# A list scheduler gets a model of two transfer queues and more slack behind transfers; the last stage's inputs lie on every second partition; the last rows are summed from PSUM

## The chip, the cores and the metric

One core of a Trainium2 chip runs the kernel. The metric is the device time of one execution in microseconds (us); the time before is the median of three runs.

## The reference

Input `x` is one sequence of 2048 rows with 512 channels. The result mixes two functions of it by a gate per row. `a` is a long convolution (an S4D state-space kernel of 128 complex states per channel, applied by a Fourier transform of twice the length), `b` is a bilinear feed-forward layer of inner width 1792 on a second input of the same shape.

```python
g = _sigmoid((x * gate_w).sum(-1, keepdims=True))
# a:
dt = jnp.exp(log_dt)
A = -jnp.exp(log_A_real) + 1j * A_imag
C = (C_real + 1j * C_imag) * dt[:, None]
P = jnp.exp((A * dt[:, None])[:, :, None] * pos[None, None, :])
K = 2.0 * jnp.einsum("dn,dnl->dl", C, P).real
y = irfft(rfft(u_t, 2 * L) * rfft(K, 2 * L), 2 * L)[:, :, :L]
a = y + u * D_skip
# b:
b = ((x_b @ w_gate) * (x_b @ w_up)) @ w_down
return g * a + (1 - g) * b
```

## The kernel before

**The feed-forward layer** is cut into 14 slices of 128 inner columns, in four groups (3, 3, 4 and 4 slices), and the rows into four chunks of 512. `hidden(f)` makes the two products `pg` and `pu` of a slice (12 TensorE matmuls each, since each operand is split into a high and a low part: `whi`, `wlo`, `xs`), copies `pg` to `h` (ScalarE), multiplies `h` by `pu` (VectorE, `h<-pu,h`), and splits the product into `hh` (ScalarE) and `hl` (VectorE). `down` adds the slices of a group up in a bank `y` of PSUM, one bank per 128 rows, two banks in all. `evacuate` scales `y` by 1 - g into `acc` (ScalarE) and adds it to the output in HBM (an accumulating transfer of the POOL queue). The weights of the next group come through two tiles `raw` (SP queue); ScalarE rounds each of them into `whi` or `dhi`, which frees the tile.

**The convolution** runs beside it on four quarters of the channels (`q`, 0 to 3), and its transform is a chain of small matmuls into banks `k`, with a trip through HBM between its steps because the data have to change partitions:

- `k_block(b)`, 16 blocks of 32 channels: VectorE builds two tables, `x` and `v`, by complex products (with squares `sq` from ScalarE); the last instruction of a block's tables is `v<-v,sq` of 32 by 8 elements per partition. Then the **kernel product** `k<-v,x` on TensorE makes the convolution kernel of these channels.
- `k_first(q)`: first step of the kernel's transform, matmuls `k<-kt,w1k_t`, stored to `sk_d`.
- `m_second`, four times per quarter: `m_load` fetches parts of `su_d` (the input's transform, made early on by `u_part` with matmuls `k<-in,w2s`) and of `sk_d` on the POOL queue; matmuls `k<-in,w2s`; ScalarE empties the banks into `ev`. `m_product` multiplies the two spectra on VectorE (`y<-ev`, `ev<-ev`, `y<-y,ev`). `m_inverse` takes two such products back (`k<-y,w3s`) and stores to `y_d` (SP queue).
- `m_last(q, gs)`: loads from `y_d` (`in<-y_d`, and `x<-y_d` in the last quarter), matmuls `k<-in,w_t` or `k<-x,w_t`, sums, the factor g, and an accumulating transfer into the output. The first four of the last chunk's row groups are kept apart: `ends()` reads their 4 x 128 output rows back into `sums` (`kt<-out`), adds the rest and stores them (`out<-kt`). These are the kernel's last instructions.

**The order of the work** is set by a list scheduler in the kernel's Python code. Every step is a task with an engine, a planned duration, inputs and outputs, a rank, for transfers a size, and for some an earliest time (`T_STEP` paces the slices). `Work.run` repeatedly takes the task that can start first by its plan, with ties by rank, and so writes out one fixed order per engine; on the chip each engine goes through its own list in that order and waits where an input is late. A transfer's end is planned in `run` by one `bus` for all transfers, which serves them one after the other at `DMA_RATE`; `ready` adds the lag between a task and its reader. `APART` keeps groups of small matmuls 6 us apart.

Every instruction is issued through one helper, so the profile gives all of them one line, L119; groups are told apart by the names of their tiles.

Of the kernel before, what the change touches and what calls it, by code (L numbers as in the profile page):

```python
# [18 lines left out]
P = 128  # L19
# [31 lines left out]
def fourier_matrices():  # L51

    k1, th = np.arange(64), 2 * np.pi / 4096

    def first(a, halves):
        re, im = np.cos(2 * np.pi * np.outer(a, k1) / 128), -np.sin(2 * np.pi * np.outer(a, k1) / 128)
        im[:, 0] = np.sin(np.pi * a)
        return np.concatenate([re, im, -re], axis=1)

    w1 = np.tile(first(np.arange(32) - 31.5, 2), (4, 1))  # L60
    rows = np.array(K_ROWS)
    w1k = np.tile(np.stack([first(2 * rows + b - 31.5, 1) for b in range(2)], 1), (4, 1, 1))
# [43 lines left out]
    w4 = w4.reshape(2, 2, 4, 2, 4, 32).transpose(0, 1, 3, 2, 4, 5)  # L106
    parts = (w1, w1k, w2.reshape(P, 32, 32), w3.reshape(P, 8, 2, 2, 64), w4.reshape(P, 32))
    return [np.ascontiguousarray(a, np.float32) for a in parts]

# [52 lines left out]
        self.deps, self.tiles, self.start, self.end, self.rows, self.many = set(), [], None, None, (), 0  # L162


class Work:


# [11 lines left out]


    APART, LESS = 6.0, 4.0
    DMA_RATE = 0.3

    def __init__(self):
        self.tags, self.tasks = {}, []
# [77 lines left out]
    def run(self):  # L263
# [4 lines left out]
        bus, order, known, rows, apart = 0.0, [], {}, {}, -9.0  # L268
# [51 lines left out]
def gated_mix_kernel(  # L320
# [260 lines left out]
    def evacuate(gi, ci, r, y):  # L581
        t = 4 * ci + r
        final = gi == len(GROUPS) - 1 and ci == LAST
        acc = new("glu", "raw", [P, D], bufs=2) if final and r == 3 else new("glu", "acc", [P, D], bufs=3)
        add(
            "act", 0.69, lambda: act.activation(acc.t, y.t, AF.Copy, scale=ngate[:, t : t + 1]),
            r=[y, (m_gate, ci)], w=[acc], rank=0,
        )
        if final:
            ending.append((r, acc))  # L590
        elif gi == 0:
            add("sp", 0.42, lambda: sp.dma_start(ov[:, t, :], acc.t), r=[acc], w=[(m_out, t)], dma=256)
        else:
            add(
                "pool", 0.95, lambda: pool_q.dma_start(ov[:, t, :], acc.t, accum_op=ALU.add),
                r=[acc, (m_out, t)], dma=640, rows=[t],
            )

    def ends():
# [2 lines left out]
        sums = new("tab", "kt", [P, 4, D])  # L602
        add(
            "sp", 0.42, lambda: sp.dma_start(sums.t, ov[:, t0 : t0 + 4, :]),
            r=[(m_y, (KT - 1, 0))], w=[sums, *((m_out, t0 + r) for r in range(4))], dma=1024, rows=range(t0, t0 + 4),
        )
        for r, acc in ending:
            t = t0 + r
            for q, (fin, parts) in late["fin"].items():
# [6 lines left out]
                    r=[*parts, (m_gate, LAST)], w=[(sums, (r, q))], rank=0,  # L616
                )
            add(
                "dve", 0.69,
                lambda r=r, acc=acc: dve.tensor_tensor(  # L620
                    out=sums.t[:, r], in0=acc.t, in1=sums.t[:, r], op=ALU.add
                ),
                r=[acc], w=[(sums, (r, q)) for q in range(KT - 2, KT)], rank=0,
            )
            add(
                "sp", 0.42, lambda r=r, t=t: sp.dma_start(ov[:, t, :], sums.t[:, r]), r=[(sums, (r, q)) for q in range(KT - 2, KT)], w=[(m_out, t)],
                dma=256, rank=-1,
            )
# [476 lines left out]
    def m_load(q, T):  # L1105
# [11 lines left out]
        for w, (src, m) in enumerate(((su_d, m_su), (sk_d, m_sk))):  # L1117
            for p in range(2):
# [6 lines left out]
                    r=[(m, (q, n0)) for n0 in range(0, 32, 8 if w else 4)], w=[(t, (T, w, p))], dma=256,  # L1125
                )
        return at, [(t, (T, w, p)) for w in range(2) for p in range(2)]

# [60 lines left out]
    def m_inverse(q, T0, ys, ws):  # L1189
# [27 lines left out]
            )  # L1217
        for h in range(2):
            st = sts[h]
            b0 = 32 * (T0 + h)  # L1220
            add(
                "sp", 0.42,
                lambda b0=b0, st=st: sp.dma_start(
                    y_d[q, b0 : b0 + 32].rearrange("(u a) n d -> (a n) u d", u=8),
                    st.t.rearrange("p t i j d -> p (t i j) d"),
                ),
                r=[st], w=[(m_y, (q, T0 + h))], dma=512,
            )


    def m_last(q, gs):

        banks, pieces, src = [[bank() for _ in range(2)] for _ in gs], [], []
        for g in gs:
            if q == KT - 1:
                t = late["y"][g]
            else:
                t = inp([P, 16, P])
                for p in range(2):
                    add(  # L1240
                        "sp", 0.42,
                        lambda t=t, g=g, p=p: sp.dma_start(
                            t.t[64 * p : 64 * p + 64],
                            y_d[q].rearrange("(k p) n d -> p k n d", p=2)[p, :, 16 * g : 16 * g + 16],
                        ),
                        r=[(m_y, (q, T)) for T in range(4)], w=[(t, p)], dma=512,
                    )
# [21 lines left out]
        for g, t, n0, n in pieces:  # L1269
# [30 lines left out]
            if n == 1 and n0 == LAST % 2:  # L1300
# [5 lines left out]
            add(  # L1306
                "pool", 0.95,
                lambda rs=rs, flat=flat: pool_q.dma_start(ov[:, rs[0] : rs[-1] + 1, cs], flat(), accum_op=ALU.add),
                r=[*parts, *((m_out, r) for r in rs)], dma=160 * len(rs), rows=rs,
            )  # L1310

    def transforms(q):
# [21 lines left out]
        if q == KT - 1:  # L1334
            late["y"] = [new("tab", "x", [P, 16, P], bufs=2) for _ in range(2)]
            for g in (1 - LAST // 2, LAST // 2):
                for half in range(2):
                    for p in range(2):
                        lanes = slice(64 * p + 32 * half, 64 * p + 32 * half + 32)
                        rows_y = y_d[q, 64 * half : 64 * half + 64].rearrange("(k p) n d -> p k (n d)", p=2)  # L1340
                        add(
                            "sp", 0.42,
                            lambda t=late["y"][g], lanes=lanes, rows_y=rows_y, p=p, g=g: sp.dma_start(
                                t.t[lanes], rows_y[p, :, 16 * P * g : 16 * P * g + 16 * P]
                            ),
                            r=[(m_y, (q, 2 * half + k)) for k in range(2)], w=[(late["y"][g], (half, p))], dma=256,
                        )
# [84 lines left out]
```

## Time and profile before

| | |
|---|---|
| median of 3 runs | 602.53 us (602.51 to 604.89) |
| the profiled execution, its own time | 601.78 us |
| its span | 600.0 us |
| mean granted TensorE clock | 0.994 |
| TensorE busy with matmuls | 585.8 us, 98% |
| VectorE, ScalarE busy | 512.3 us (85%), 401.0 us (67%) |
| moved by transfers | 137.33 MB, 229 GB/s on average |

The page gives busy time per engine, the share of busy time in 40 slices of the span, the transfers by queue, the chain of waits that ended last, and the costliest groups. A row of a group or of the timeline reads: engine, operation, output tile <- input tiles, shape, count, and in brackets how long the engine was idle before it and what released it. TensorE issues a 512-column matmul every 0.23 us, although each is listed with about 0.39 us, because they overlap.

### The profile page before, as it was taken

The page shows a single profiled execution, that of the slowest core. Times are in us where ns is not written, and L with a number is a line of the kernel's source. Part 1 is how long each engine was busy: PE and PEld are TensorE (multiplying, and loading weights), DVE is VectorE, ACT ScalarE, POOL GpSimd, SP SyncE. Part 2 cuts the span into 40 slices and gives each one's busy share as a digit, 9 for nine tenths or more (in the row PEclk, how much of TensorE's full clock was granted, in tenths as well). Part 3 has the DMA queues.
Part 4 walks back from the last instruction along what each step waited for, and adds up shares of the span by engine and source line. Part 5 has one row for each costly group of instructions (what it writes and reads, how often), then busy time and mean ns, then how long its engine had stood idle before and what let it go on. Part 6 is the DMA issues. An engine that isn't in the chain of part 4 may idle for free.

```text
span 600.0 us, 15878 instructions
## 1 busy us (share of the span) xinstructions
PE 585.8 (98%) x6500; PEld 443.4 (74%) x6500; DVE 512.3 (85%) x811; ACT 401.0 (67%) x893; POOL 128.9 (21%) x191
## 2 busy tenths in 40 slices
PE   8899999999999999999999999999999999999996
PEld 5657777777877787887777877866878777767674
DVE  6999999999998997999999999978999933486525
ACT  5279787999678479967959764979984423433522
POOL 0011212221204131310133301104353023201111
PEclk9989999999999999999999999999999999999998
DMA  8899979699869699996959945999999569959976
GB/s 276 314 357 340 336 281 338 187 207 253 232 175 227 166 241 248 195 229 163 302 135 266 215 129 171 226 250 239 182 203 260 95 159 355 244 153 264 279 141 122
DMA packets 71867, 137.33 MB, mean 229 GB/s; under 512 B 7156, under 2 KB 35828, under 8 KB 69364
## 3 DMA queue, kind: packets, MB, share of 16 engines
q1 hardware_dynamic: 47476, 88.21, 45.9%
q0 software_dynamic: 23904, 47.98, 40.4%
q8 instruction: 51, 0.84, 0.6%
q10 hardware_dynamic: 416, 0.13, 0.1%
q14 instruction: 20, 0.16, 0.1%
HBM read 81.25 MB, written 55.05 MB: 227 GB/s over the span
## 4 chain that ended last, share of the span: by engine, by line
PE 79%; DVE 8%; ACT 6%; DMA 5%; issue 1%; ACTq 0%; DVEq 0%
PE y L119 22%; PE pu L119 21%; PE pg L119 21%; PE k L119 15%; DMA raw<-in_wts 4%; DVE x L119 2%; DVE y L119 1%; DVE v L119 1%; ACT ts L119 1%; ACT whi L119 1%; DMA y<-in_xT 1%; ACT L119 1%; DVE h L119 1%; DVE t L119 1%; DVE xs L119 1%
## 5 line engine op out<-in xcount | busy, mean ns | idle before, releaser
L119 PE MATMUL pg<-xs,whi 128*128 128x512 f32 x448 | 139.2, 392 | 1.0 <-DVE xs L119 0.7
L119 PE MATMUL pu<-xs,whi 128*128 128x512 f32 x448 | 138.7, 391 | 0.0
L119 PEld LDWEIGHTS pg<-xs,whi 128*128 128x128 f32 x448 | 84.5, 189 | 20.0 <-ACT whi L119 2.0
L119 PEld LDWEIGHTS pu<-xs,whi 128*128 128x128 f32 x448 | 84.4, 188 | 17.1
L119 PE MATMUL y<-dhi,hl 128*128 128x512 f32 x224 | 90.5, 404 | 2.2 <-DVE x L119 1.1
L119 PE MATMUL pu<-xs,wlo 128*128 128x512 f32 x224 | 90.1, 402 | 0.9 <-issue 0.5
L119 PE MATMUL pg<-xs,wlo 128*128 128x512 f32 x224 | 90.1, 402 | 0.8 <-ACT whi L119 0.5
L119 PE MATMUL y<-dlo,hh 128*128 128x512 f32 x224 | 87.5, 391 | 1.3 <-DVE dlo L119 1.3
L119 PE MATMUL y<-dhi,hh 128*128 128x512 f32 x224 | 87.4, 390 | 0.0
L119 POOL DMA_DIRECT2D out<-acc x44 | 38.4, 954 | 184.8 <-ACT acc L119 173.8
L119 ACT COPY ev<-k 128x512 f32<-128x512 f32 x112 | 59.2, 595 | 15.7 <-PE k L119 15.6
L119 ACT CAST hh<-h 128x512 fp32r<-128x512 f32 x56 | 34.7, 620 | 43.3 <-DVE h L119 43.2
L119 ACT ACTIVATE acc<-y,ngate 128x512 f32<-128x512 f32 x63 | 42.8, 686 | 30.6 <-PE y L119 28.2
L119 DVE TENSOR_TENSOR h<-pu,h 128x512 f32<-128x512 f32 x56 | 38.6, 689 | 23.0 <-PE pu L119 22.2
L119 PEld LDWEIGHTS y<-dhi,hl 128*128 128x128 f32 x224 | 42.0, 188 | 21.7 <-issue 6.2
L119 PEld LDWEIGHTS pu<-xs,wlo 128*128 128x128 f32 x224 | 42.1, 188 | 19.2 <-issue 9.8
L119 PEld LDWEIGHTS pg<-xs,wlo 128*128 128x128 f32 x224 | 42.0, 188 | 19.1 <-issue 6.8
L119 ACT COPY h<-pg 128x512 f32<-128x512 f32 x56 | 33.1, 590 | 29.7 <-PE pg L119 27.8
L119 PEld LDWEIGHTS y<-dlo,hh 128*128 128x128 f32 x224 | 42.1, 188 | 9.5 <-DVE dlo L119 1.7
L119 PEld LDWEIGHTS y<-dhi,hh 128*128 128x128 f32 x224 | 42.1, 188 | 9.1
L119 DVE TENSOR_TENSOR hl<-h,hh 128x512 fp32r<-128x512 f32 x56 | 38.5, 687 | 8.4 <-ACT hh L119 8.4
L119 POOL DMA_DIRECT2D su_d<-ev x32 | 17.3, 549 | 90.2 <-ACT ev L119 90.2
(127 smaller groups left out, 1015.7 us busy)
## 6 DMA issues: line engine op xcount, KB each, us to landing
xs<-xs_d SPq DMA_DIRECT2D x36, 512.0 KB, 7.8
out<-acc POOLq DMA_DIRECT2D x44, 256.0 KB, 7.1
raw<-in_wts SPq DMA_DIRECT2D x36, 256.0 KB, 5.2
xs_d<-xs SPq DMA_DIRECT2D x16, 512.0 KB, 7.1
su_d<-ev POOLq DMA_DIRECT2D x32, 256.0 KB, 5.3
y_d<-ts SPq DMA_DIRECT2D x14, 512.0 KB, 6.5
in<-su_d POOLq DMA_DIRECT2D x24, 256.0 KB, 8.4
sk_d<-ev SPq DMA_DIRECT2D x6, 1024.0 KB, 6.2
```

The source lines that it names most:

```text
L119: got = getattr(self.engine, name)(*args, **kw)
```

## The change

Five things are edited.

1. The planner's transfers. `Bus` replaces the single `bus`: two queues, one for POOL and one for SP and ScalarE, each served in order, both at half the rate while both have work. `DMA_RATE` goes from 0.30 to 0.34, and times from issue to start (`SENT`) and from last byte to reader (`LANDED`) are given per queue. Sizes in the plan are set anew: 554 for 640 (`evacuate`), 476 for 256 (`m_load`), 203 for 160 per row group (`m_last`). None of these numbers is seen by the chip but through the order.
2. Slack: after 20 us of plan, a TensorE, ScalarE or VectorE task is planned no earlier than 1 us (`SURE`) after the transfer that it needs.
3. `y_d` rows lie on partitions another way: `w3` and `w4` are permuted on the host, `m_inverse` stores each staging tile by two transfers of 64 partitions (every second one), and the last stage's loads fill every second partition, with 64 each, where they filled 64 neighbouring ones (or 32 in the last quarter, which then has 4 loads of 512 KB for 8 of 256 KB). In quarters 0 to 2 a load now needs one half of the rows of `y_d`, stored by one `m_inverse` (`half`), where it needed all.
4. `ends()`: rows 2 and 3 of the last chunk are no longer copied to `acc` or `raw` by ScalarE; VectorE scales and adds them from PSUM in one instruction.
5. The very last row group is done in two halves of 256 columns, stored by SP and by the ScalarE queue.

```diff
+class Bus:
+    def __init__(self):
+        self.now, self.queues = 0.0, ([], [])
+
+    def serve(self, queues, now, until):
+        done = []
+        while now < until and any(queues):
+            share = sum(map(bool, queues))
+            step = min([q[0][1] * share for q in queues if q] + [until - now])
+            now += step
+            for q in queues:
+                if q:
+                    q[0][1] -= step / share
+                    if q[0][1] < 1e-6:
+                        done.append((q.pop(0)[0], now))
+        return done
...
-    DMA_RATE = 0.3
+    DMA_RATE = 0.34
+    SENT = {"sp": 0.9, "act": 0.9, "pool": 1.4}
+    LANDED = {"sp": 1.0, "act": 1.0, "pool": 1.3}
+    SURE = 1.0
...
         if d.engine == task.engine == "pe":
             return d.end
+        if d.dma and d.start > 20.0 and task.engine in ("pe", "act", "dve"):
+            return d.end + self.SURE
...
             if t.dma:
-                bus = max(bus, t.end + 1.3) + t.dma / self.DMA_RATE / 1000
-                t.end = bus + 0.5
+                for d, end in bus.add(t, t.end - 0.42 + self.SENT[t.engine], t.dma / self.DMA_RATE / 1000):
+                    d.end = end + self.LANDED[d.engine]
...
         final = gi == len(GROUPS) - 1 and ci == LAST
-        acc = new("glu", "raw", [P, D], bufs=2) if final and r == 3 else new("glu", "acc", [P, D], bufs=3)
+        if final and r > 1:
+            ending.append((r, y))
+            return
+        acc = new("glu", "acc", [P, D], bufs=3)
...
+            for n, cs in enumerate((slice(0, D // 2), slice(D // 2, D)) if r == 3 else (slice(0, D),)):
...
+                    scale = 1.0 if r < 2 else ngate[:, t : t + 1]
+                    dve.scalar_tensor_tensor(
+                        sums.t[:, r, cs], acc.t[:, cs], scale, sums.t[:, r, cs], op0=ALU.mult, op1=ALU.add
+                    )
+                e, q = ("act", act) if n else ("sp", sp)
...
-                    y_d[q, b0 : b0 + 32].rearrange("(u a) n d -> (a n) u d", u=8),
-                    st.t.rearrange("p t i j d -> p (t i j) d"),
+                        y_d[q, b0 : b0 + 16].rearrange("(u e) n d -> (e n) u d", u=8),
+                        st.t[p::2].rearrange("p t i j d -> p (t i j) d"),
...
+    def halves(q, t, g, half):
+        rows_y = y_d[q, 64 * half : 64 * half + 64].rearrange("r n d -> r (n d)")
+        sp.dma_start(t.t[half::2].rearrange("p n d -> p (n d)"), rows_y[:, 16 * P * g : 16 * P * g + 16 * P])
```

The new plan gives another order on every engine from start to end. Three places follow.

TensorE, around the 11th of the 16 kernel products `k<-v,x`, in the third group of slices; `pu_4595` and `pg_4573` are the products of that group's second slice (its low weights are `wlo_2985`). Before:

```order
L119 MATMUL pg_4573<-xs_4107,wlo_2985 128x512
L119 MATMUL pg_4573<-xs_4107,whi_2966 128x512 x2
L119 MATMUL pu_4595<-xs_4091,wlo_2985 128x512
L119 MATMUL pu_4595<-xs_4091,whi_2966 128x512 x2
L119 MATMUL k_4607<-v_662,x_3904 32x64 x64
L119 MATMUL pu_4595<-xs_4101,wlo_2985 128x512
```

After, where `pg_4536` and `pu_4560` belong to the first slice of that group (`wlo_2859`):

```order
L120 MATMUL pg_4536<-xs_4177,wlo_2859 128x512
L120 MATMUL pg_4536<-xs_4177,whi_2848 128x512 x2
L120 MATMUL pu_4560<-xs_4156,wlo_2859 128x512
L120 MATMUL pu_4560<-xs_4156,whi_2848 128x512 x2
L120 MATMUL k_4576<-v_671,x_3966 32x64 x64
L120 MATMUL pu_4560<-xs_4172,wlo_2859 128x512
```

The product has moved ahead by one slice: 12 `pg` and 12 `pu` matmuls that stood before it now stand behind it, and all else ahead of it is the same in number.

VectorE, the instructions up to the last one of the same block's tables (`v<-v,sq` of 32x8, the last row; what stands ahead of these rows is, but for one `hl`, the same in sum). Before:

```order
L119 TENSOR_TENSOR h<-pu,h 128x512
L119 SCALAR_TENSOR_TENSOR v<-v 128x32x16
L119 TENSOR_TENSOR ri<-rt,e 128x672
L119 TENSOR_TENSOR v<-v,sq 128x32x16
L119 TENSOR_TENSOR hl<-h,hh 128x512
L119 SCALAR_TENSOR_TENSOR v<-v 128x32x8
L119 TENSOR_TENSOR v<-v,sq 128x32x8
```

After:

```order
L120 SCALAR_TENSOR_TENSOR v<-v 128x32x16
L120 TENSOR_TENSOR ri<-t,e 128x672
L120 TENSOR_TENSOR ri<-rt,e 128x672
L120 TENSOR_TENSOR t<-pb,turns 128x672
L120 TENSOR_TENSOR v<-v,sq 128x32x16
L120 TENSOR_TENSOR su<-ri 128x576
L120 SCALAR_TENSOR_TENSOR v<-v 128x32x8
L120 TENSOR_TENSOR h<-pu,h 128x512
L120 TENSOR_TENSOR y<-ev 128x1024
L120 TENSOR_TENSOR v<-v,sq 128x32x8
```

Four instructions that came later now come first (`ri<-t,e`, `t<-pb,turns` and `su<-ri`, which prepare the next block, and `y<-ev` of the spectra's product), and one `hl` fewer stands ahead of the last row.

SP queue, where the weights of the fourth group begin to load while the second quarter's last stage does (`in<-y_d`). Before:

```order
L119 DMA pb<-par_d 128x64 x2
L119 DMA in<-y_d 64x2048 x3
L119 DMA raw<-in_wts 128x512
L119 DMA in<-y_d 64x2048
L119 DMA raw<-in_wts 128x512 x2
L119 DMA sk_d<-ev 128x2048
```

After:

```order
L120 DMA pb<-par_d 128x64 x2
L120 DMA in<-y_d 64x2048 x2
L120 DMA raw<-in_wts 128x512 x2
L120 DMA sk_d<-ev 128x2048
L120 DMA raw<-in_wts 128x512 x2
```

Of the four loads from `y_d` that stood among the first weight tiles, two have moved further up the queue, ahead of four `xs` loads: they fetch the rows that the quarter's first `m_inverse` stored.

More of the change, by code (lines that the diff above doesn't have):

```diff
@@ L104, in fourier_matrices @@
         w4[0, 0], w4[1, 0] = 1.0, np.sin(np.pi * a)
-    w4 = w4.reshape(2, 2, 4, 2, 4, 32).transpose(0, 1, 3, 2, 4, 5)
+    w3 = w3.transpose(0, 1, 2, 3, 4, 6, 5)
+    w4 = w4.reshape(2, 2, 4, 2, 4, 32).transpose(0, 3, 2, 4, 1, 5)
     parts = (w1, w1k, w2.reshape(P, 32, 32), w3.reshape(P, 8, 2, 2, 64), w4.reshape(P, 32))
@@ L162, in __init__, with add @@
         self.deps, self.tiles, self.start, self.end, self.rows, self.many = set(), [], None, None, (), 0
+class Bus:
[13 more added lines that the diff above has]
+        return done
+    def add(self, task, at, us):
+        at = max(at, self.now)
+        self.serve(self.queues, self.now, at)
+        self.now = at
+        self.queues[task.engine == "pool"].append([task, us])
+        return self.serve([[[*x] for x in q] for q in self.queues], at, 1e9)
 class Work:
@@ L267, in run @@
         free = {e: 0.0 for e in left}
-        bus, order, known, rows, apart = 0.0, [], {}, {}, -9.0
+        order, known, rows, apart = [], {}, {}, -9.0
+        bus, then = Bus(), {}
+        for t in self.tasks:
+            for d in t.deps:
+                if d.dma:
+                    then.setdefault(d, []).append(t)
         while any(left.values()):
@@ L305, in run @@
             if t.dma:
-                bus = max(bus, t.end + 1.3) + t.dma / self.DMA_RATE / 1000
-                t.end = bus + 0.5
+                for d, end in bus.add(t, t.end - 0.42 + self.SENT[t.engine], t.dma / self.DMA_RATE / 1000):
+                    d.end = end + self.LANDED[d.engine]
+                    for x in then.get(d, ()):
+                        known.pop(x, None)
             rows.update((r, t.end) for r in t.rows)
@@ L595, in evacuate @@
                 "pool", 0.95, lambda: pool_q.dma_start(ov[:, t, :], acc.t, accum_op=ALU.add),
-                r=[acc, (m_out, t)], dma=640, rows=[t],
+                r=[acc, (m_out, t)], dma=554, rows=[t],
             )
@@ L604, in ends @@
             "sp", 0.42, lambda: sp.dma_start(sums.t, ov[:, t0 : t0 + 4, :]),
-            r=[(m_y, (KT - 1, 0))], w=[sums, *((m_out, t0 + r) for r in range(4))], dma=1024, rows=range(t0, t0 + 4),
+            r=[(m_y, (KT - 1, 0, 0))], w=[sums, *((m_out, t0 + r) for r in range(4))], dma=1024, rows=range(t0, t0 + 4),
         )
@@ L615, in ends, with total @@
                     ),
-                    r=[*parts, (m_gate, LAST)], w=[(sums, (r, q))], rank=0,
+                    r=[*parts, (m_gate, LAST)], w=[(sums, (r, 1))], rank=0,
                 )
[L618 to L628, printed above, removed]
+            for n, cs in enumerate((slice(0, D // 2), slice(D // 2, D)) if r == 3 else (slice(0, D),)):
+                part = [(sums, (r, k)) for k in (range(2) if r < 3 else (n,))]
+                def total(r=r, t=t, acc=acc, cs=cs):
+                    scale = 1.0 if r < 2 else ngate[:, t : t + 1]
+                    dve.scalar_tensor_tensor(
+                        sums.t[:, r, cs], acc.t[:, cs], scale, sums.t[:, r, cs], op0=ALU.mult, op1=ALU.add
+                    )
+                add("dve", 0.42 if r == 3 else 0.69, total, r=[acc, (m_gate, LAST)], w=part, rank=0)
+                e, q = ("act", act) if n else ("sp", sp)
+                add(
+                    e, 0.42, lambda r=r, t=t, cs=cs, q=q: q.dma_start(ov[:, t, cs], sums.t[:, r, cs]), r=part,
+                    dma=128 if r == 3 else 256, rank=-1,
+                )
     def glu():
@@ L1124, in m_load @@
                     ),
-                    r=[(m, (q, n0)) for n0 in range(0, 32, 8 if w else 4)], w=[(t, (T, w, p))], dma=256,
+                    r=[(m, (q, n0)) for n0 in range(0, 32, 8 if w else 4)], w=[(t, (T, w, p))], dma=476,
                 )
@@ L1238, in m_last @@
                 t = inp([P, 16, P])
[L1239 to L1247, printed above, removed]
+                for half in range(2):
+                    add("sp", 0.42, lambda t=t, g=g, half=half: halves(q, t, g, half), r=y_parts(q, half), w=[(t, half)], dma=512)
             src.append(t)
@@ L1308, in m_last @@
                 lambda rs=rs, flat=flat: pool_q.dma_start(ov[:, rs[0] : rs[-1] + 1, cs], flat(), accum_op=ALU.add),
-                r=[*parts, *((m_out, r) for r in rs)], dma=160 * len(rs), rows=rs,
+                r=[*parts, *((m_out, r) for r in rs)], dma=203 * len(rs), rows=rs,
             )
@@ L1337, in transforms @@
                 for half in range(2):
[L1338 to L1347, printed above, removed]
+                    t = late["y"][g]
+                    add("sp", 0.42, lambda t=t, g=g, half=half: halves(q, t, g, half), r=y_parts(q, half), w=[(t, half)], dma=512)
         for q, gs in {KT - 2: [], KT - 1: [(q - 1, (0, 1)), (q, (1 - LAST // 2,)), (q, (LAST // 2,))]}.get(q, [(q, (0, 1))]):
```

17 lines of the change are left out of this document (10 added, 7 removed).

## The prediction

> **What bounds the kernel now.** I read the page first, then what TensorE waited for, then busy time by stretches of the span, and last the timeline at the places where a wait begins.
>
> From the page:
>
> ```profile
> span 600.0 us, 15878 instructions
> PE 585.8 (98%) x6500; PEld 443.4 (74%) x6500; DVE 512.3 (85%) x811; ACT 401.0 (67%) x893; POOL 128.9 (21%) x191
> ```
>
> TensorE (PE) is the bound: it lacks 14.2 us of the span, and the change takes no matmul from it. So all that can be won is idle time of TensorE, and a part of that is fixed: the time before its first inputs land, and 5.6 us behind its last matmul (the row at 594.38 below). Two of its waits:
>
> ```profile
> PE y L119 <- DVE dlo L119: 1.3, 1, 1.3
> PE pu L119 <- DVE h L119: 0.4, 1, 0.4
> ```
>
> No row of that answer names a transfer. Transfers reach TensorE by a detour: ScalarE waits for one, VectorE for ScalarE, TensorE for VectorE. Busy time by stretches:
>
> ```profile
> 25.00:30.00 5.00, 2.60 (x11) 1.61 (x10) 4.96 (x13) 1.40 (x3) 0.00 (x0) 1.00 0.55 143
> 30.00:34.00 4.00, 3.45 (x10) 2.24 (x9) 3.95 (x10) 2.42 (x10) 0.00 (x0) 0.57 0.99 395
> 100.00:150.00 50.00, 49.27 (x461) 38.85 (x460) 47.59 (x72) 45.17 (x98) 11.49 (x17) 1.00 0.89 235
> 400.00:450.00 50.00, 49.18 (x587) 37.04 (x585) 46.28 (x71) 44.90 (x107) 20.22 (x25) 1.00 0.99 216
> 520.00:560.00 40.00, 39.72 (x741) 29.72 (x725) 25.99 (x37) 14.52 (x26) 3.44 (x4) 1.00 0.88 223
> ```
>
> The columns are TensorE, its weight loads, VectorE, ScalarE, POOL, the granted clock and the transfers' share. In the first part VectorE is a second bound: it is busy 47.59 and 46.28 of 50 us, and the kernel products wait for its tables. From 520 us on it has time to spare (25.99 of 40). TensorE's idle time between start and end is 2.4 us at 25 to 30, 0.7 at 100 to 150, 0.8 at 400 to 450, 0.3 at 520 to 560.
>
> **The change, part by part.** The sum is made against the profiled execution, 601.78 us with a span of 600.0; the median of the runs is 602.53, 0.75 above it, and I carry differences over to the median.
>
> *The last rows.* Today's end:
>
> ```profile
> 594.38 0.69 ACT L119 ACTIVATE raw<-y,ngate 128x512 f32<-128x512 f32 x1 [2.03 <-PE y L119]
> 595.10 0.69 DVE L119 TENSOR_TENSOR kt<-raw,kt 128x512 f32<-128x512 f32 x1 [2.02 <-ACT raw L119]
> 595.82 0.33 SPq L119 DMA_DIRECT2D out<-kt  x1
> L119 DVE TENSOR_TENSOR x<-k,x 128x256 f32<-128x256 f32 x4 | 1.4, 416 | 0.0
> y<-in_xT SPq DMA_DIRECT2D x4, 256.0 KB, 4.6
> ev<-in_wts ACTq DMA_DIRECT2D x1, 128.0 KB, 4.3
> ```
>
> The last sum starts 0.72 us after ScalarE and ends at 595.79; the store takes the remaining 4.2 us. After the change ScalarE's step is gone and VectorE starts at about 594.38 on the first 256 columns. The nearest row for 256 columns out of a PSUM bank is `x<-k,x`, 416 ns; two make 0.83, so the last half is ready at 595.2 in place of 595.8: minus 0.6. A 128 KB transfer landed 0.3 us sooner than one of 256 KB: minus 0.3. Issuing on ScalarE's queue may take 0.1 longer. Taken: **minus 0.8**. Between minus 1.4 (the halves overlap fully) and 0 (two stores at once, each with its own fixed time, end no sooner than one). Row 2's own instruction is hidden: VectorE was idle 2.02 us before the last row.
>
> *The start.* Two u products (`k<-in,w2s`) and one slice meet late inputs:
>
> ```profile
> 37.83 2.22 PE L119 MATMUL k<-in,w2s 32*64 32x512 f32 x16
> 42.93 1.11 PE L119 MATMUL k<-in,w2s 32*64 32x512 f32 x16
> 45.13 0.73 PE L119 MATMUL pg<-xs,whi 128*128 128x512 f32 x2 [0.65 <-DVE xs L119]
> ```
>
> The first u product takes 1.1 us longer than the second, which is a wait inside it. In the new order 6 matmuls of a slice come ahead of it, so that this wait has cover; and the fourth `xs` stands one `y<-in` earlier on VectorE, but TensorE gets there earlier too. Taken: **minus 0.6**; between minus 1.8 (both waits go) and 0. The waits for `dlo` at 25 to 30 us keep their instructions in the same order, so I leave them.
>
> *Weights behind fewer loads.* The clearest case of the detour:
>
> ```profile
> 384.36 2.32 SPq L119 DMA_DIRECT2D in<-y_d  x3
> 387.85 13.48 DMA raw<-in_wts
> 401.35 0.62 ACT L119 CAST whi<-raw 128x512 fp32r<-128x512 f32 x1 [1.61 <-DMA raw<-in_wts]
> 403.07 0.69 DVE L119 TENSOR_TENSOR v<-v,sq 128x512 f32<-128x512 f32 x1 [1.48 <-ACT sq L119]
> ```
>
> The weight tile landed 13.48 us after its issue, behind four loads of 512 KB; ScalarE waited 1.61 us for it with the squares queued behind, VectorE 1.48 us for those. TensorE's 0.4 us for `h` comes right behind that, and the stretch has 0.8 us of its idle time. In the new order only two of these loads stand ahead of that tile. Taken: this idle time goes, **minus 0.8**; between minus 1.5 (the 0.7 at 100 to 150 too) and 0.
>
> *Kernel products against VectorE.* The scheduler now puts them earlier among the slices. For the 11th and the 12th the trace shows when the tables are done and when TensorE begins:
>
> ```profile
> 347.50 0.66 DVE L119 TENSOR_TENSOR v<-v,sq 128x256 f32<-128x256 f32 x1
> 354.74 2.06 PE L119 MATMUL k<-v,x 128*32 128x64 f32 x128
> 379.46 0.63 DVE L119 TENSOR_TENSOR v<-v,sq 128x256 f32<-128x256 f32 x1
> 381.26 1.95 PE L119 MATMUL k<-v,x 128*32 128x64 f32 x122
> 350.73 2.72 PE pg L119 x12
> L119 DVE TENSOR_TENSOR ri<-t,e 128x672 f32<-128x672 f32 x16 | 13.7, 855 | 0.8 <-ACT t L119 0.7
> L119 DVE TENSOR_TENSOR su<-ri 128x576 f32<-128x576 f32 x16 | 12.1, 756 | 0.2
> L119 DVE TENSOR_TENSOR t<-pb,turns 128x672 f32<-128x672 f32 x15 | 12.8, 854 | 0.0
> L119 DVE TENSOR_TENSOR y<-ev 128x1024 f32<-128x1024 f32 x16 | 19.5, 1220 | 14.6 <-ACT ev L119 8.3 <-PE k L119 6.0
> L119 DVE TENSOR_TENSOR hl<-h,hh 128x512 fp32r<-128x512 f32 x56 | 38.5, 687 | 8.4 <-ACT hh L119 8.4
> ```
>
> 11th: the tables end at 348.16, the product starts at 354.74, 6.6 us of slack. In the new order 24 slice matmuls fewer stand ahead of it; 12 take 2.72 us, so TensorE comes 5.4 us earlier, at 349.3. VectorE has `ri<-t,e`, `su<-ri`, `t<-pb,turns` and `y<-ev` more and one `hl` less ahead of the tables' end: 0.86 + 0.76 + 0.85 + 1.22 - 0.69 = 3.0 us, so they end at 351.1. TensorE is 1.8 us short. 12th: 18 matmuls fewer (4.1 us), one `t<-pb,turns` fewer (0.85 us): 377.2 against 379.2, 2.0 us short. These are not added, since a wait at the 11th delays TensorE at the 12th too: 2.0 together if VectorE idles elsewhere as it does now. It may idle less, its wait for late squares being a part of it. Taken: **plus 1.6**, between 0 and 2.0 on these rows, more only if VectorE is held up anew (second rival).
>
> *Edits at nothing.* The permuted `w3` and `w4` have the same shapes. SP issues 16 stores more and 4 loads fewer; it waits most of the span. Between the last `m_inverse` and the first `k<-x,w_t`, the shortest such trip, the new order has 96 slice matmuls, 21.8 us, as cover for the stores (93 before, and TensorE did not wait).
>
> The loads onto every second partition I cost at nothing too:
>
> ```profile
> xs<-xs_d SPq DMA_DIRECT2D x36, 512.0 KB, 7.8
> in<-y_d SPq DMA_DIRECT2D x12, 512.0 KB, 7.7
> ```
>
> 512 KB onto 64 neighbouring partitions landed as soon as onto 128. The Trainium skill says otherwise ("SBUF — State Buffer", section "Door 1: The DMA port swizzle"): 64 neighbouring partitions reach half of the 16 ports and were measured at 196 GB/s against 328 for all 128; every second partition would reach all. By that page a load would end an estimated 1.1 us sooner, and the sum would stay as it is, because no wait of TensorE ends with such a load; it would only speak for the first rival.
>
> The sum: -0.8 - 0.6 - 0.8 + 1.6 = -0.6. That is 601.2 us for the profiled execution and **601.9 us** for the median.
>
> **The rivals.** About 0.5%, 3 us, is what a measurement of this kernel can tell from no change: 599.5 and 605.5 are the borders.
>
> *First rival, faster.* The plan's better transfers take away nearly all waits, VectorE's tables come in time: -0.8 - 0.6 and the idle time from 100 us on (0.7 + 0.8 + 0.3), and TensorE is no longer left idle at 25 to 30 us. That idle time costs twice now: after it the clock was granted at 0.57 over 4.0 us, 1.7 us of work lost. Sum: -4.9, so 597.6. For it: the detour through ScalarE is plain in the rows. Against it: the instructions at 25 to 30 us are in the same order, and the kernel products have less slack than before. The Trainium skill's rule here ("TensorE: Matmul & The Clock Gate", "Part 1: The HAM clock gate") is that an idle window of about 3.4 us brings half clock until a busy one has passed; the trace agrees with the half clock, though TensorE was idle only 2.4 of those 5 us.
>
> *Second rival, slower: VectorE's tables come late.* The 11th product's slack of 6.6 us is used up, and any hold of VectorE ahead of it now reaches TensorE in full. One such stretch as at 400 to 450 us (3.7 us idle on VectorE) ahead of the 11th product adds 3.7 to the 2.0: -0.8 - 0.6 + 5.7 = +4.3, 606.8. It decides from the point where VectorE is held 2.4 us longer ahead of that product than now. For it: transfers and ScalarE's list are reshuffled everywhere. Against it: the plan knows VectorE's durations well, so late weights would have to cause it.
>
> *Third rival: the last quarter's kernel arrives late.*
>
> ```profile
> 493.72 2.00 PE L119 MATMUL k<-kt,w1k_t 32*128 32x512 f32 x16
> 497.26 0.32 SPq L119 DMA_DIRECT2D sk_d<-e  x1
> sk_d<-e SPq DMA_DIRECT2D x1, 512.0 KB, 8.0
> x<-sk_d POOLq DMA_DIRECT2D x4, 256.0 KB, 8.3
> L119 POOL DMA_DIRECT2D x<-sk_d x4: 778/818/1183, 507.5 to 510.2; - x4
> 525.82 1.49 PE L119 MATMUL k<-x,w2s 32*32 32x256 f32 x64
> ```
>
> From `k_first` to the first use of its result TensorE has 32 us of work today. The new order leaves 72 slice matmuls (16.3 us) and three small groups, about 22.7. The trip needs 3.5 to the issue, 8.0, about 1.6 for two issues on POOL, 8.3: 21.4. It fits by 1.3; with transfers 2 to 5 us slower TensorE waits up to 4: 601.9 to 605.9.
>
> *Fourth: the new plan does nothing that TensorE notices*, since it never waited for transfers; only the end is won, -0.8: 601.7.
>
> **How the numbers follow.** The forecast (600.0 to 604.5; all low bounds together are the first rival's ground) gets 0.55, the first rival 0.15, the second 0.17, the third 0.08 (0.05 of it beyond 605.5), the fourth 0.05. So faster by over 0.5%: 0.15; slower by over 0.5%: 0.17 + 0.05 = 0.22; the rest, 0.63, within. A range from 598.5 to 606.5 leaves out about half of the first and of the second rival and keeps the rest.
>
> **What would show it.** Right: no `raw` ahead of the last store, and about 4.9 us from TensorE's last matmul to the end in place of 5.6; a wait of TensorE's `k` for VectorE's `v` of 1 to 2 us at the 11th or 12th kernel product; the weight tile beside the second quarter's last loads landing in under 10 us. Wrong: waits for `v` or `ev` summing to over 4 us, idle time before `k<-x,w2s`, or waits in the first 46 us that differ by over 1 us from today's.

## The result: 610.41 us, and the profile after

The changed kernel took 610.41 us (median; 608.99 to 611.63) against 602.95 us of the kernel before beside it: a ratio of 1.0117, 95% interval 1.0081 to 1.0152. That is 1.2% slower, clear of the noise, 8.5 us above the predicted 601.9 and outside its range. Medians are over all executions; ratios leave out those in a slower state of the chip, which is one in all (605.77 us, of the best order below). The profiled execution of the changed kernel, 611.63 us with a span of 609.9, is read here. From its page:

```profile
span 609.9 us, 15894 instructions
PE 588.6 (97%) x6500; PEld 446.6 (73%) x6500; DVE 512.5 (84%) x812; ACT 399.0 (65%) x891; POOL 128.9 (21%) x191
```

The span grew by 9.9 us. TensorE's idle time rose from 14.2 to 21.3 us (7.1), and its busy time by 2.8 us with no matmul added, so it ran slower for some time. What it waited for (us in total, times, longest):

```profile
PE y L120 <- ACT acc L120: 5.8, 2, 3.8
PE pu L120 <- issue: 2.5, 1, 2.5
PE pg L120 <- ACT xs L120: 2.2, 1, 2.2
...
PE pg L120 <- ACT h L120: 1.3, 1, 1.3
PE k L120 <- DVE v L120: 0.9, 1, 0.9
```

Three of these five name ScalarE (ACT), which the prediction never had as what releases TensorE from a long wait. Busy time by stretches, with the columns and three of the windows of before, and two of the stretches at half clock:

```profile
100.00:150.00 50.00, 46.19 (x411) 36.19 (x414) 43.89 (x66) 42.87 (x91) 12.66 (x18) 0.97 0.85 214
130.50:134.00 3.50, 3.50 (x9) 2.81 (x10) 3.50 (x5) 2.57 (x6) 0.00 (x0) 0.55 0.86 221
280.40:284.30 3.90, 3.90 (x11) 3.04 (x12) 3.32 (x8) 2.40 (x9) 0.00 (x0) 0.58 0.57 235
400.00:450.00 50.00, 46.73 (x501) 35.24 (x500) 40.70 (x65) 40.71 (x100) 14.99 (x17) 1.00 0.98 216
520.00:560.00 40.00, 40.00 (x661) 30.23 (x639) 26.14 (x37) 15.00 (x28) 5.26 (x7) 1.00 0.91 260
```

TensorE is idle for 3.8 us at 100 to 150 (0.7 before) and 3.3 us at 400 to 450 (0.8 before), both in stretches in which weight tiles are loaded; in the last part it loses nothing. The 2.5 us marked "issue" stand apart, at 278 us, and are no wait for weights (last section). The wait of 3.8 us, on ScalarE's and TensorE's timeline:

```profile
126.38 0.62 ACT L120 CAST dhi<-raw 128x512 fp32r<-128x512 f32 x1 [4.62 <-DMA raw<-in_wts]
...
129.75 1.25 ACT L120 ACTIVATE acc<-y,ngate 128x512 f32<-128x512 f32 x2
130.47 0.50 PE L120 MATMUL y<-dhi,hl 128*128 128x512 f32 x1 [3.81 <-ACT acc L120]
```

ScalarE takes its list in order. The cast `dhi<-raw` found its weight tile not there and stood 4.62 us; `acc<-y`, which empties the PSUM bank that TensorE wants, stood behind it though its own input was ready. The two tiles issued at 116 to 117 us took this long to land, a row on the tile `raw` in that window:

```profile
DMA to landing us min/median/max: 10.3/11.1/12.0
```

The chain of waits puts this place down to `pb<-par_d`, a table's input that by the chain landed at 127.9 us; the first experiment speaks against it. The same shape stands at 427 and 447 us, and at 43 us with a store in the tile's place. In the chain of waits (start, us, what):

```profile
33.15 7.92 DMA out<-acc
...
41.18 0.69 ACT acc L120
...
414.27 11.24 DMA raw<-in_wts
...
435.91 9.84 DMA raw<-in_wts
```

All of ScalarE's waits for these weight tiles, first in the kernel before, then in the changed one:

```profile
ACT whi L119 <- DMA raw<-in_wts: 3.4, 2, 1.8
ACT dhi L119 <- DMA raw<-in_wts: 2.4, 2, 1.2
```

```profile
ACT dhi L120 <- DMA raw<-in_wts: 9.7, 5, 4.6
...
ACT whi L120 <- DMA raw<-in_wts: 3.1, 2, 2.6
```

5.8 us became 12.8. The tiles do not land that much later. From issue to landing, between 85 and 460 us, before and then after:

```profile
DMA to landing us min/median/max: 2.6/4.9/13.5
```

```profile
DMA to landing us min/median/max: 2.7/6.0/12.0
```

The plan calls for them sooner. Worked out from the planner's own rules, not measured: from planned issue to planned landing a weight tile behind 85 us takes 7.7 us in the old plan (median) and 4.4 in the new one, to which the new rule adds 1 us of slack. The old plan was pessimistic by some 3 us, and that was its margin.

### The profile page after: what moved, and what is told of

Its sections match the earlier page's. It is cut to its first block, busy times and chain, and to the rows that moved or that the text cites. A ratio compares the mean times of both kernels' runs of the same rounds, so it can differ in the third digit from the quotient of the medians.

```text
span 609.9 us, 15894 instructions
## 1 busy us (share of the span) xinstructions
PE 588.6 (97%) x6500; PEld 446.6 (73%) x6500; DVE 512.5 (84%) x812; ACT 399.0 (65%) x891; POOL 128.9 (21%) x191
## 4 chain that ended last, share of the span: by engine, by line
PE 81%; DMA 9%; DVE 5%; ACT 3%; issue 1%; SPq 0%; DVEq 0%; ACTq 0%
PE y L120 22%; PE pg L120 22%; PE pu L120 21%; PE k L120 15%; DMA raw<-in_wts 5%; DMA out<-acc 1%; DMA w3s<-in_rows 1%; DMA pb<-par_d 1%; DVE v L120 1%; DVE x L120 1%; DMA ev<-in_wts 1%; ACT acc L120 1%; DVE y L120 1%; SPq L120 0%; DVE dlo L120 0%
## 5 line engine op out<-in xcount | busy, mean ns | idle before, releaser
L120 PE MATMUL pg<-xs,whi 128*128 128x512 f32 x448 | 140.9, 396 | 0.7 <-ACT whi L120 0.5
L120 PE MATMUL pg<-xs,wlo 128*128 128x512 f32 x224 | 91.5, 409 | 3.6 <-ACT xs L120 2.2
L120 POOL DMA_DIRECT2D out<-acc x44 | 39.7, 971 | 208.7 <-ACT acc L120 191.5
```

The lines of the kernel that those rows point to most:

```text
L120: got = getattr(self.engine, name)(*args, **kw)
```

## The experiments

Theory A: the new plan calls for weight tiles before they have landed, ScalarE's list stands behind them, and TensorE behind ScalarE. Theory B: the new layout makes transfers late. Theory C: the new order is worse whatever its slack. Theory D: with so little margin some transfer is late in any order, and the weight tiles are only this order's. Ratios are to the kernel before on the same chip, in brackets the 95% interval.

**The wait for weights taken out of the changed kernel.** From the second group on ScalarE's casts read a constant, `w1k_t`, which is loaded earlier for it (`to()` is the same place in `hi`; the code is shortened, and in the last group VectorE's rests read the constant too). The order is unchanged and the weights are still loaded, but nothing reads their tiles, so a load no longer waits for a cast: the two of 116.09 us start at 111.59.

```diff
-act.copy(hi.t[:, c * D : (c + 1) * D], t.t)      # t: the loaded raw tile
+act.copy(to(), w1k_t[:, 0:1, :P].to_broadcast([P, 4, P]))
```

> The changed kernel, instruction for instruction in the same order, but from the second group on ScalarE's casts of weights (and in the last group VectorE's rest) read a constant that lies in SBUF since 80 us in place of the loaded tile; the loads still run. The weights of these groups are thereby wrong numbers. Only the wait for the loads is gone. Theory A: the gaps at 126, 427, 447 and 465 us go (4.0 + 2.1 + 1.4 + 1.0, and about 2 of half clock): 600 to 604 us. If late weight tiles are not the cause: 608 us or more.

599.96 us, 0.9957 [0.9936, 0.9979]: as theory A has it. Against the changed kernel's 1.0117 that is 1.60%, 9.6 us. The place of the 3.8 us wait again, on ScalarE's timeline:

```profile
122.48 0.62 ACT L120 CAST dhi<-w1k_t 128x512 fp32r<-128x512 f32 x1
...
125.85 1.25 ACT L120 ACTIVATE acc<-y,ngate 128x512 f32<-128x512 f32 x2
```

`acc` comes 3.9 us earlier, TensorE does not wait there, and `pb<-par_d` holds nobody: issued at 122.17 in place of 121.32 us, it lands 5.8 us later, after `acc` has begun. Two gaps stayed: 2.8 us for `xs` at 44 us, and 1.8 us without a releaser at 275 us.

**The same edit in the kernel before.**

> The kernel before, in its own order, with the same constant read in place of the loaded weight tiles from the second group on (weights of these groups are wrong numbers). Theory A: the old plan left hardly any such wait, so little is to be won: 601 to 602.5 us, 0.5 to 1.5 below the kernel before, against the 10 us that the same edit was worth in the changed order. If the edit gains by itself (a cast that reads another place, or a load that nobody waits for): 597 us or less.

599.29 us, 0.9945 [0.9927, 0.9964]. More than expected: the edit is worth 0.55%, 3.3 us, in the old order and 9.6 in the new one. How much of the 3.3 us is late tiles, and how much the edit's own (its loads start earlier), is not shown. If the edit's own gain is alike in both orders, which was not tried, it drops out of the difference. That difference, 6.3 us (about 3 either way by the intervals), is most of the loss of 1.17%, 7.1 us. Without these waits the two orders are level: 0.9957 and 0.9945, 0.7 us, within the intervals.

**Plan alone, layout and last rows alone.** The two halves of the diff.

> The kernel before with the changed plan alone (two queues, the new rate and sizes, 1 us of slack), loads and stores laid out as before, last rows as before. Theory A (the plan lets ScalarE's list stand behind weight tiles that have not landed): 608 to 613 us, at least two waits of TensorE for ScalarE's acc, h or xs of over 1 us, each with a raw tile behind it. Theory B (the new layout of loads and stores makes transfers late): 601 to 604 us.

626.66 us, 1.0372 [1.0314, 1.0431]. The plan is the culprit, but the size is missed: with the old layout and last rows it loses some 16 us more than the changed kernel, whose planner is the same but whose order is another. The profiled execution (620.17 us; the timed ones are 6.5 longer, and no trace shows why) has ScalarE waiting 15.6 us for weight tiles, 5.1 us of waits of TensorE without a releaser, and 10.5 us from its last matmul to the end.

> The other half: the new layout and the last rows from PSUM, with the plan as before. Theory A: 600 to 602.5 us, 0.8 of it from the last rows, no wait of TensorE for acc of over 1 us. Theory B: 606 us or more.

601.37 us, 0.9978 [0.9957, 0.9998], with no wait for `acc`: theory B falls. The two halves do not add up to the whole (1.0372 and 0.9978 against 1.0117), since each combination gives an order of its own; what a plan costs is not a fixed number.

**Layout alone.**

> The kernel before with the new layout of loads and stores alone (half tiles, every second partition), in the old plan. Together with the last rows it measured 0.9978 of the kernel before, the last rows alone 0.9998: 601 to 602.5 us, loads of the second quarter's y tiles landing in 4 to 6 us against 7.7.

0.9982 [0.9957, 1.0007]; the median, 602.82 us, is that of before. Perhaps 1 us, not shown. What is plain is the landing; the load's rows in this run and in the changed kernel:

```profile
in<-y_d SPq DMA_DIRECT2D x12, 512.0 KB, 6.2
```

```profile
in<-y_d SPq DMA_DIRECT2D x12, 512.0 KB, 4.6
```

7.7 us before. Over all traces this load's median is 7.3 to 9.7 us in the five orders with the old layout, and 4.6 to 6.5 us in the eleven with the new one, but for 7.6 in the run with 6 us of slack for every `raw` tile. The Trainium skill's rule on ports ("SBUF — State Buffer", section "Door 1: The DMA port swizzle"), from which the prediction worked out that every second partition reaches all of them, was right in sign, and the prediction was wrong to weigh it down by the 7.7 and 7.8 us of two different loads. No wait of TensorE ends with such a load, so little came of it.

**Last rows alone.**

> The kernel before with the last rows alone as in the changed kernel (rows 2 and 3 from PSUM, the last store in two halves on two queues), in the plan as before. The prediction gave 0.8 us for it; the changed kernel's trace has 3.7 us from TensorE's last matmul to the end against 5.6 before, which would be 1.9 us: 601.1 us against 602.2 by the prediction.

602.35 us, 0.9998 [0.9985, 1.0011]: nothing. The last store of before, then the two halves in this run and the last half in the changed kernel (KB each, us to landing):

```profile
out<-kt SPq DMA_DIRECT2D x1, 256.0 KB, 2.8
```

```profile
out<-kt SPq DMA_DIRECT2D x1, 128.0 KB, 3.5
out<-kt ACTq DMA_DIRECT2D x1, 128.0 KB, 3.4
```

```profile
out<-kt ACTq DMA_DIRECT2D x1, 128.0 KB, 1.7
```

The last store is issued at 594.82 in place of 595.82, but from there to the end it is 4.7 us (599.5) in place of 4.2: the stores of the other rows still drain beside it. In the changed kernel the last transform came 11 us ahead of the end of the slices in place of 8, these stores were out, and the end took 3.7 us (606.18 to 609.9) in place of 5.6.

**Slack of 4 us for all transfers, and of none.** In the rule for `pe`, `act` and `dve`, `SURE = 4.0`; in the second run the rule is taken out.

> The changed kernel with 4 us of slack in place of 1 for what needs a transfer. The landing that the plan expects of a weight tile is then about as late as the old plan had it. Theory A: 601 to 605 us, and the waits for acc, h and xs sum to under 3 us. Theory C (the new order itself is worse, whatever the slack: kernel products packed against VectorE's tables): 608 us or more. If slack is given back by work that starts later, between the two.

608.69 us, 1.0103 [1.0071, 1.0135]: a miss, for a reason of its own. ScalarE waits only 0.9 us for weight tiles, and TensorE's last work ends at 592.4 us, 13.8 us before that of the changed kernel. But then, on its timeline:

```profile
589.14 0.39 PE L120 MATMUL y<-dhi,hh 128*128 128x512 f32 x1
590.07 2.30 PE L120 MATMUL k<-x,w_t 64*32 64x512 f32 x32 [0.54 <-DMA x<-y_d]
```

The last transform stands behind all slices, and nothing covers its sums and stores: the end comes 14 us later. By its time alone this run speaks for theory C (608 us or more). Two later runs decide against C: 4 us for weight tiles after 80 us, and 3 us for all transfers in the plan's middle.

> The changed kernel with 4 us of slack for transfers that are planned to start before 520 us, and 1 us after it. With 4 us everywhere TensorE had few waits up to 589 us, but its last product (k<-x,w_t) came behind all slices, at 590 us, and 16.2 us of work that nothing covers followed it. Theory A (late weight tiles behind ScalarE's list are the loss, slack cures it, and the end was what 4 us everywhere cost): 597 to 601 us. If an order of this plan is slower whatever its slack: 605 us or more.

608.73 us, 1.0104 [1.0082, 1.0125]. The cure of the end failed: the slack of the transfers before 520 us had already moved the last transform there (it starts at 590.22 us). The interior is clean again (0.5 us of ScalarE's waits).

> The changed kernel without the slack of 1 us (the rule of the old plan, 0.03 to 0.3 us, in its place). Theory A and D: more waits behind transfers than with 1 us, 611 to 625 us. If the slack itself moved the work badly: 605 us or less.

613.14 us, 1.0159 [1.0132, 1.0187]. The time is as expected, the waits are not: ScalarE's waits for weight tiles are 6.1 us, fewer than the 12.8 of the changed kernel, and its last transform, too, stands at 593.5 us, behind all but a few of the slices' matmuls. This run does not test theory A.

**Slack for loaded tiles alone.** First 6 us for every `raw` tile, then 4 us for those planned after 80 us:

```diff
-            return d.end + self.SURE
+            return d.end + (4.0 if d.start > 80.0 and d.tiles and d.tiles[0].tag == "raw" else self.SURE)
```

> The changed kernel, 1 us of slack as in it, but 6 us for what reads a loaded weight or input tile (raw) alone. Theory A: ScalarE's list no longer meets a weight tile that has not landed; 600 to 604 us, and TensorE's waits for acc and h under 2 us together. If late weight tiles are only a sign of a crowded bus: 607 us or more.

626.70 us, 1.0399 [1.0360, 1.0439]: a miss of 23 us. Its waits for weight tiles are gone (0.8 us). But the slack also held the input tiles of the first 80 us: by the planner's own times the slices then end 16 us later (596 in place of 579), before any transfer is late. The plan itself was worse.

> The changed kernel with 4 us of slack for weight tiles that are planned after 80 us, and 1 us for all other transfers; the first 80 us and the plan's end stay nearly as in the changed kernel (the plan puts the last product k<-x,w_t 12 us ahead of the end of the slices, as in the changed kernel; with 4 us for all it stood behind them). Theory A (late weight tiles are the loss, and slack for them alone cures it): TensorE's waits for acc and h after 100 us sum to under 1.5 us, 599 to 603 us. Theory D (with 1 us of slack any order of this plan meets some transfer late, the weight tiles were only the ones of this order; the run with 6 us for input and weight tiles alone, 626.7 us, speaks for it): 607 us or more, with waits on xs, k or y in other places.

600.89 us, 0.9963 [0.9941, 0.9986]: 1.54%, 9.3 us, below the changed kernel by one number of the plan, as theory A has it and against D. ScalarE's wait for the weight tiles, and TensorE's for `h`:

```profile
ACT dhi L120 <- DMA raw<-in_wts: 1.5, 2, 0.9
PE pg L120 <- ACT h L120: 1.6, 2, 1.4
```

There is no wait for `acc` any more, and the 1.6 us for `h` are just above the 1.5 expected. What is left besides is the 2.5 us for `xs` at 45 us. Theory C falls with this run: an order of the new plan is no slower than the old one.

**3 us for all transfers between 80 and 440 us.**

> The changed kernel with 3 us of slack for every transfer planned between 80 and 440 us, 1 us outside; the last product stands 12 us ahead of the slices' end in the plan. Theory A and theory D both: few waits between 80 and 450 us; 597 to 602 us, as the waits of TensorE were gone there with 4 us everywhere and only the end was spoilt. If it is 606 us or more though the end is as in the changed kernel, slack is no cure.

603.55 us, 1.0010 [0.9991, 1.0028]. The waits for weight tiles are gone (0.6 us), and the loss with them, but 2.0 us for an `xs` tile at 512 us and 2.5 us without a releaser came in: 1.5 us above the range expected.

**Slack for early stores too.** To the 4 us for weight tiles, 4 us for stores of `acc` planned before 80 us.

> As the run with 4 us of slack for weight tiles after 80 us, and also 4 us for stores of acc planned before 80 us. Theory A on a store: the wait of TensorE for xs at 43 to 45 us (2.2 to 2.8 us, ScalarE held behind a store that still reads its acc buffer) goes or falls under 1 us, the half clock after it too: 597 to 600.5 us. If that wait has another cause, it stays over 2 us and the time at 600 to 602.

598.88 us, 0.9927 [0.9908, 0.9946]: faster than both kernels, and the best that was found. ScalarE's wait for the store, in the run before it and in this one:

```profile
ACT acc L120 <- DMA out<-acc: 5.0, 2, 3.0
```

```profile
ACT acc L120 <- DMA out<-acc: 0.7, 1, 0.7
```

The wait for `xs` is gone, as it should be if the same mechanism acted on a store. But ScalarE's waits for weight tiles are back to 4.8 us from 1.5 (three casts) in this best order, so their sum alone does not tell the time: such a wait costs where something that TensorE needs stands behind it. Waits of 1.6 us (`acc`, 33 us) and 1.4 us (`ev`, 44 us) stand in the place of the one for `xs`, and TensorE's work in the first 50 us (busy time by granted clock) is only 0.6 us ahead; where the rest of the 2.2 us comes from is open, and a difference of that size between two orders may be chance (last section).

**The old plan with its margin taken.** One number, `DMA_RATE = 0.4` in place of `0.3`; the rest as before.

> The kernel before with one number changed: the old one-queue plan takes transfers at 0.40 in place of 0.30, so that it plans weight tiles 3.9 us after their issue (median) in place of 7.7; layout and last rows as before. Theory A (margin): waits of TensorE for acc, h or xs with a raw tile behind them, 605 to 615 us. If the two-queue form of the new plan is what hurts, and not its shorter landings: 600 to 603.5 us.

629.57 us, 1.0444 [1.0413, 1.0475]. The one-queue plan, told that weight tiles land after 3.9 us, loses more than the changed kernel does. So it is not the two-queue form that hurts. The size is beyond what was expected, and weight tiles are not all of it. ScalarE's and TensorE's waits:

```profile
ACT dhi L119 <- DMA raw<-in_wts: 7.7, 7, 3.9
ACT xs L119 <- DMA raw<-in_xT: 6.3, 4, 2.5
```

```profile
PE k L119 <- issue: 8.2, 5, 3.0
PE k L119 <- DMA in<-y_d: 2.3, 2, 1.3
```

TensorE's busy time is 595.0 us, 9.2 above that of before, with a mean granted clock of 0.981 in place of 0.994: most of it is half clock. Here theory D holds as well: with the margin of all transfers gone, inputs and loads of `y_d` come late too.

## Why the prediction was wrong, step by step

*Weights behind fewer loads (minus 0.8): the step that failed, in sign and size.* It took one tile that would have fewer loads ahead, and gave the whole stretch that gain. On that tile it held: the two weight tiles behind the second quarter's last loads, issued at 398.9 and 399.4 us, landed after 2.8 us each, against 13.48 in the kernel before. But the two issued at 413.3 and 414.3 us, with none of these loads ahead of them, took 8.2 and 11.2 us, and ScalarE stood for the second. What the plan believes of a landing was not worked out at all, though the rate, `SENT`, `LANDED` and `SURE` in the diff give it: 7.7 us before, 4.4 and 1 of slack after. The runs put about plus 6.3 in its place. The detour it reckoned with (ScalarE, VectorE, TensorE) was not the path either: TensorE waits for ScalarE directly. The answer on the kernel before, of which the prediction shows two rows, had this in small:

```profile
PE y L119 <- ACT acc L119: 0.9, 2, 0.6
PE pg L119 <- ACT whi L119: 0.9, 2, 0.5
```

*Kernel products (plus 1.6): did not come.* In the order with the weight waits taken out, the 11th product has its tables at 351.73 and starts at 353.34:

```profile
351.11 0.62 DVE L120 TENSOR_TENSOR v<-v,sq 128x256 f32<-128x256 f32 x1
353.34 2.07 PE L120 MATMUL k<-v,x 128*32 128x64 f32 x128
```

VectorE was forecast at 351.1 and came within 0.6 us; TensorE was forecast at 349.3 and lost 4 us on the way, to waits that this step did not have (2.80 us for `xs` and 1.78 us of "issue", with half clock behind each). So VectorE's time was right, and it was these other losses, not slack in the tables, that kept TensorE from waiting there. In the changed kernel TensorE's one wait for `v`, 0.9 us, is at the 15th.

*The start (minus 0.6): wrong in sign.* TensorE waits 2.2 us for `xs` at 43 us, behind the store that landed after 7.92 us, and half clock follows (0.51 over 3.5 us from 45.5 us, 1.7 us of work). Against the 1.1 and 0.65 us that were to go, that is an estimated plus 2. The prediction named idle time before `k<-in,w2s` and looked at VectorE's order; ScalarE's list and the `acc` buffers were not looked at.

*The last rows (minus 0.8): the trace of the changed kernel gives 1.9, the edit alone 0.* The price of the last store (0.3 sooner for half the bytes) forgot the stores beside it.

*Edits at nothing:* the layout is worth between minus 2.6 and plus 0.4 us by its interval, which holds nothing; its landing was mis-sized by 1.5 to 3.1 us.

*The rivals.* The second named the right cause, "late weights would have to cause it", with the wrong path: through VectorE to the 11th product. The path was ScalarE's list to `acc`, `h` and `xs`, without VectorE, and its price was not bounded by one product. The third did not occur: no wait of TensorE after 467 us is over 0.6 us. The first rival's sum has a slip: of the idle time at 25 to 30 us it takes off the half clock (1.7) but not the 2.4 us themselves; with them it would be minus 7.3, 595.2 us.

*The clock.* After the waits of 3.81 and 2.50 us the clock was granted at 0.55 over 3.5 us and at 0.58 over 3.9 us, 1.6 us of work lost each time. It was also halved after the 2.24 us at 43 us, as said, but not after the wait of 1.98 us at 429 us:

```profile
429.00:433.00 4.00, 3.87 (x17) 3.20 (x18) 2.57 (x4) 2.90 (x9) 0.78 (x1) 1.00 1.12 242
```

So three waits cost 1.6 to 1.7 us more than their length here. The length alone does not decide: in the run with 3 us between 80 and 440 us, 1.00 was granted from 43.5 to 48 us, behind a wait of 2.21 us, and 0.50 from 513.7 to 517.1 us, behind one of 1.99. The prediction used this for the faster rival only, and not for what a new wait would cost.

## What to carry to other kernels

When a change gives a list scheduler better transfer times, ask first what margin the worse ones held: with engines that take their lists in order, a tile that lands late holds everything behind it, and a plan that is right on the median is too early for half of the tiles. Put the slack on the transfers whose consumer stands ahead of work that the bound engine waits for, not on all: slack on every transfer moved the last transform behind the work that had covered its stores. And price an end by what still drains beside the last store, not by that store alone.

## What was not expected of the hardware

In nearly every order TensorE stood for nothing that the profile names ("issue"): 2.5 us in the changed kernel, 5.1 with the plan alone, 9.3 in seven waits in the last experiment, 0.3 in the best, at most 4.5 us at a time. The traces show what it stood for. In the changed kernel, on TensorE's timeline, and the instruction queue's row, of the window of 276 to 281 us and of the whole page (pieces, MB, share):

```profile
280.37 0.50 PE L120 MATMUL pu<-xs,whi 128*128 128x512 f32 x1 [2.50 <-issue]
q8 instruction: 1, 0.02, 1.2%
q8 instruction: 51, 0.84, 0.6%
```

The queue moves 51 pieces of 16 KB, and TensorE's list has 13128 records (matmuls, weight loads, semaphores), about 256 to a piece. The piece in this window starts at 278.11 us, with TensorE already idle, and lands at 279.04; 1.33 us later TensorE goes on. The timelines of all kernels here list 28 "issue" waits of TensorE. Of these, 26 end 1.26 to 1.59 us after such a piece has landed, and at a record whose number is 193 to 196 above a multiple of 256 (here 5314, or 20 times 256 and 194). So TensorE waited for its own next instructions. Two waits of the last experiment (0.69 and 2.07 us) do not fit and stay open.

These waits belong to an order and are not chance: without the weight waits, in the same order, the same matmul waits again, 1.78 us. Why a few of the pieces are sent for too late is not shown. The one here follows a kernel product, whose 128 matmuls and 128 weight loads take TensorE 2.07 us; most kernel products pass without such a wait. A new order moves them, as it moves single late transfers (2.0 us for an `xs` tile at 512 us), and one of them can be worth 4 us (2.50, and 1.6 of half clock, here). So a difference of 2 to 3 us between two orders, by itself, says little about a plan.
